# Two transformer layers on one core: VectorE jobs held back until their data has landed, sums called back one run earlier, single projections as 64x32 tiles

## The chip, the cores and the metric

The kernel runs on one core of a Trainium2 chip. The metric is the device time of one execution in microseconds (us); where several runs were made, their median. The core's engines are named as in the profile: PE (TensorE, matmuls), PEld (its weight loads), DVE (VectorE), ACT (ScalarE), POOL (GpSimd) and SP, whose queue issues the DMAs, one after the other; a DMA that must wait for a semaphore holds those behind it.

## The reference

Two equal layers are applied to x, 2048 rows of 512 numbers in float32. Each has an attention with 32 heads of width 16, whose keys and values are shared by all heads, and a dense part of width 1792 with ReLU. The weights of both layers are the same tensors.

```
def _A_ref(x, wq, wk, wv, wo):
    q = (x @ wq).reshape(B, S, H, Dh).transpose(0, 2, 1, 3)
    k = x @ wk
    v = x @ wv
    scores = jnp.einsum("bhqd,bkd->bhqk", q, k) * (Dh ** -0.5)
    p = _softmax(scores, axis=-1)
    o = jnp.einsum("bhqk,bkd->bhqd", p, v)
    return o.transpose(0, 2, 1, 3).reshape(B, S, H * Dh) @ wo

def _B_ref(x, w1, w2):
    return jnp.maximum(x @ w1, 0) @ w2

x = x + _A_ref(_layernorm(x), wq, wk, wv, wo)
x = x + _B_ref(_layernorm(x), w1, w2)
x = x + _A_ref(_layernorm(x), wq, wk, wv, wo)
x = x + _B_ref(_layernorm(x), w1, w2)
```

## The kernel before

**Units and steps.** The rows are cut into four blocks (b) of 512. The attention of a layer is cut into 32 units U (64 in all): a unit is one block's queries for four heads, eight units to a block. A unit walks over 16 key tiles (kt) of 128 keys; one unit and one key tile are a step, 1024 steps in all. Of each step `scores` makes two halves: eight matmuls of 64x32 tiles on the 512 columns of the queries into PSUM (`fst`), and one ACT call that takes the exponential of 1024 columns into `fp`. `values` then multiplies `fp` by the values into two accumulators (`facc`). Two matmuls of this kind, on the two halves of the 128 rows, and four column groups run as eight small tiles side by side; `tiles` (L263) writes one half of them.

**The end of a unit.** `keep` (L1069) adds the two accumulators into an SBUF tile `faccs` (five rotating buffers, which raw weights use too). `unit_out` (L1094) stores it to DRAM (`fod`). After an odd unit three jobs follow at fixed numbers of steps: `unit_sums` (L1101) loads the sums of the softmax (`flsum`) and the outputs (`foraw`) from there; `unit_inverse` (L1111) checks the sums on DVE, takes the reciprocal, and sends it through DRAM (`frd`) to be read back spread over the rows (`frinv`); `unit_norm` (L1125) multiplies outputs by `frinv` on DVE and splits them into two float16 parts (`fot`). Inverse and norm lie 9 and 14 steps behind the unit's end, 7 and 12 at the end of a block, 3 and 6 for unit 31 (L1447). At the end of a block `fetch` (L795) loads the rows of the residual and the first weights, and `follow` (L1394) adds that block's `chain` to the list of dense work.

**Spilled sums.** Units 32 to 41, the first of layer 1, are walked twice (`order`, L1207): over key tiles 0 to 11, and, once all are through, over 12 to 15, since the last keys of layer 1 come late. In between `spill` (L1085) stores their sums to DRAM and `recall` (L1089) loads them again; `product` (L1417) calls `recall` at the first value product of a run, and `keep` needs the sums four steps later.

**Dense work.** `chain` (L827) is the output projection, the norm (stats on DVE and POOL, halves sent through transposing DMAs), and the dense part of one block, and in layer 0 the keys and queries of layer 1 from its rows. `batch` (L268) makes two jobs at a time in 64x32 tiles, both halves of the contraction side by side in two PSUM banks (`fmisc`, which has two buffers). A job that comes alone goes another way: `mm3` (L256) makes twelve full 128x128 matmuls into one bank. Alone come the keys of each block (`key_rows`, L493, for three blocks in `following`, L712, and four in the chains of layer 0) and the queries of three groups in `following`. `key_columns` (L506) transposes the keys afterwards.

**The order of the work.** The program is written out in one order by a planner that keeps an account of the chip's time (`_Account`): each instruction and DMA is put on its engine's clock, at the end of what it needs, with modelled durations (`duration`, L132; a DMA has an issue time, a landing time LAND and bytes by FLOW, L48). `timed` (L1238) chooses by a search over the next moves whether PE next gets half a step's scores, a step's value product, or a piece of dense work, whose rate follows the due step of its chain (CHAINS, L38). Scores run at most four steps ahead of products (AHEAD). After each product, `after` (L1440) does the jobs that stand on the list of that step. One job is already held back: `unit_norm` goes to the next step while an earlier chain has not yet read `fot` (L1456). Weights come raw in the first stage: every third step from 28 on, `form` (L1401) loads one, and six steps later DVE and POOL split it into float16 parts and store it (`parts`).

A second, exact version of the net stands behind a branch at the end and is not run on these inputs.

Of the kernel before, what the change touches and what calls it, by code (L numbers as in the profile page):

```python
# [18 lines left out]
P = 128  # L19
S = 2048  # L20
D = 512
# [25 lines left out]
SIZE = {F32: 4, F32R: 4, F16: 2, I32: 4}  # L47
LAND, ISSUE, TURNED, FLOW = 1.5, 0.5, 1.25, 180e3  # L48
HOP = 0.2


class _Account:

    def __init__(self, clear=0.0):
        self.at = {"ACT": 0.0, "DVE": 0.0, "POOL": 0.0, "SP": 0.0, "PE": 0.0}
        self.slots, self.turns, self.uses = {}, {}, {}

    def place(self, t, name, bufs):
# [7 lines left out]

    def box(self, a):
        slot, pitch = self.slots.get(a.tensor.name, (None, 0))
        if slot is None:
# [17 lines left out]
    def after(self, eng, aps, writes):  # L87
        t = 0.0
        for a in aps:
            b = self.box(a)  # L90
            if b:
                for w, e, p, q, lo, hi, far, inner, end in self.uses.get(b[0], ()):
                    if (w or writes) and p < b[2] and b[1] < q and lo < b[4] and b[3] < hi:
                        if far and far == b[5] and (lo % far >= b[3] % far + b[6] or b[3] % far >= lo % far + inner):
                            continue
                        t = max(t, end + (0.0 if e == eng else HOP if e != "DMA" else 0.1))
        return t

    def note(self, eng, a, writes, end):
        b = self.box(a)  # L100
        if b:
            old = self.uses.get(b[0], [])
            floor = self.at["PE"] - 200.0
            kept = [u for u in old if u[8] > floor and not (
                (writes or not u[0] and u[1] == eng) and b[1] <= u[2] and u[3] <= b[2] and b[3] <= u[4] and u[5] <= b[4] and
                (not b[5] or b[5:] == u[6:8] and b[3] % b[5] == u[4] % b[5]))]
            self.uses[b[0]] = kept + [(writes, eng) + b[1:] + (end,)]

# [21 lines left out]


def duration(eng, op, out, ins):  # L132
    n = max(cost_of(a) for a in [out] + ins)
    psum = any(a.space == bass.MemoryType.PSUM for a in [out] + ins)
    if eng == "PE":
        n = cost_of(out)
        if op == "transpose":
            return 0.15
        c = n * (4 if ins[1].dtype == F32 else 1) / 2376.0
        return c / 8 if count(ins[0]) == 64 and cost_of(ins[0]) == 32 else c  # L140
    if eng == "ACT":
# [14 lines left out]
class _Engine:  # L156
# [4 lines left out]
    def __getattr__(self, op):  # L161
        fn = getattr(self.eng, op)

        def call(*a, **k):
# [26 lines left out]
class _Net:  # L191
# [229 lines left out]
    def forms(self):  # L421

        def wo(c):
# [3 lines left out]
            def form():  # L427
                self.until(lambda: self.exact or self.haveq[0, 3] == 4)
                self.parts(self.wo2[0][:, c], self.wo2[1][:, c], raw, 2, c)
            return form  # L430

        def w(m, f):
            raw = self.weight(m, f, False)
            return lambda: self.split(m, f, raw, False)

# [56 lines left out]

    def key_rows(self, L, b, to=None):  # L493
        nc = self.nc
# [4 lines left out]
        kop = self.kop[L][:, b * D:(b + 1) * D]  # L499
        for r in (0, 64):  # L500
            nc.vector.tensor_copy(kop[r:r + 48], kv[r:r + 48])
        for r, eng in ((32, nc.vector), (96, nc.gpsimd)):
            eng.tensor_sub(kop[r:r + DH], kv[r:r + DH], _f(kop[r:r + DH]))
        return kv

# [628 lines left out]


    def add(self, gen, size, deadline):
        self.gens.append([gen, float(size), deadline])
# [199 lines left out]
    def run(self):  # L1337
# [102 lines left out]
        def after(i):  # L1440
# [113 lines left out]
```

## Time and profile before

| | |
|---|---|
| runs, us | 2301.7, 2294.03, 2293.97; median 2294.03 |
| profiled execution, us | 2298.09 |
| its span, first to last instruction, us | 2296.3 |
| mean granted PE clock | 0.991 |
| matmuls fp x va, `facc` | 16384 records, 1130.4 us busy |
| matmuls of scores, `fst` | 16384 records, 918.8 us busy |
| ACT exponentials, 128x1024 | 2048, 1034 ns each, 1937.9 us busy |
| DMA, mean busy share of the 16 engines by queue q1 | 26.8% |

All instructions of the net are issued by one helper, so nearly every row of the profile has line L165, and groups are told apart by their tiles: out<-in, with an f in front of the program's names. A row of the timeline has the start in us from the span's start, the length, the engine, the operation and the number of instructions merged; the bracket is the engine's idle time before and what ended it. The ends of matmuls are modelled, and matmuls overlap, so PE's busy time is not PE at its peak; the time from one group's start to the next group's start is the better measure.

### The profile page before, as it was taken

How to read it: one execution, taken by the hardware profiler on the slowest of the kernel's cores; microseconds unless marked ns; L12 is line 12 of the kernel's file. 1: busy time of each engine (PE TensorE's matmuls, PEld its weight loads, DVE VectorE, ACT ScalarE, POOL GpSimd, SP SyncE). 2: the span in 40 equal slices, each digit the busy share in tenths (PEclk: the TensorE clock that was granted, in tenths of full speed). 3: DMA queues.
4: the chain of work that ended last, by engine and by line, in shares of the span. 5: the costliest groups of instructions: out<-in, count | busy, mean ns of one | idle time of the engine just before them, and what ended most of it. 6: DMA issues, size and time to landing. Idle time of an engine off the chain costs nothing.

```text
span 2296.3 us, 122379 instructions
## 1 busy us (share of the span) xinstructions
PE 2209.2 (96%) x57709; PEld 1277.0 (56%) x57709; DVE 704.2 (31%) x1533; ACT 1963.1 (85%) x2094; POOL 266.5 (12%) x311
## 2 busy tenths in 40 slices
PE   8989999999999999999899999899999999999988
PEld 4444455556566656764477754447665555555533
DVE  7433423213322233223232233332223222222242
ACT  5899999999998988777988889889999999999710
POOL 5355510001200012001010010100000000100000
PEclk9999999999999999999999999999999999999999
DMA  5344423212331133312231123432124212312032
GB/s 144 111 134 150 133 83 99 66 40 58 92 104 57 48 99 63 100 59 63 65 107 57 38 66 117 143 95 66 38 82 105 66 48 67 93 40 77 18 125 71
DMA packets 178362, 188.87 MB, mean 82 GB/s; under 512 B 79112, under 2 KB 113336, under 8 KB 177592
## 3 DMA queue, kind: packets, MB, share of 16 engines
q1 hardware_dynamic: 177848, 180.95, 26.8%
q8 instruction: 453, 7.42, 1.4%
q14 instruction: 61, 0.50, 0.1%
HBM read 116.62 MB, written 49.54 MB: 72 GB/s over the span
## 4 chain that ended last, share of the span: by engine, by line
PE 77%; ACT 13%; DMA 3%; DVE 2%; issue 2%; POOL 2%; SPq 1%; ACTq 0%; POOLq 0%; DVEq 0%
PE fmisc L165 31%; PE facc L165 30%; PE fst L165 16%; ACT fp L165 13%; DMA frinv<-frd 1%; DMA frd<-flsum 1%; DMA faccs<-fspill 1%; SPq L165 1%; POOL fxp L165 1%; POOL fbmv L165 1%; DVE fxt L165 0%; DVE fbst L165 0%; POOL fkop L165 0%; DMA out_dram<-fxt 0%; DMA fw<-fwd 0%
## 5 line engine op out<-in xcount | busy, mean ns | idle before, releaser
L165 ACT ACTIVATE fp<-fst 128x1024 f32<-128x1024 f32 x2048 | 1937.9, 1034 | 203.5 <-PE fst L165 193.8
L165 PE MATMUL facc<-fp,fva 64*32 64x512 f32 x16384 | 1130.4, 593 | 10.1 <-DVE faccs L165 6.8
L165 PE MATMUL fst<-fqop,fkop 64*32 64x512 f16 x16384 | 918.8, 378 | 41.0 <-ACT fp L165 31.3
L165 PEld LDWEIGHTS <-fkop 64*32 64x32 f16 x16384 | 387.3, 91 | 557.7 <-issue 461.0
L165 PEld LDWEIGHTS facc<-fp,fva 64*32 64x32 f32 x16384 | 364.8, 107 | 127.2 <-issue 47.5
L165 PE MATMUL fmisc<-fw,fhh 64*32 64x512 f16 (+1 forms) x6384 | 306.7, 376 | 4.5 <-DVE fseen L165 1.9
L165 PEld LDWEIGHTS <-fw 64*32 64x32 f16 (+1 forms) x9576 | 213.2, 93 | 109.4 <-issue 37.5
L165 PE MATMUL fmisc<-fxt,fw 64*32 64x512 f16 (+1 forms) x5544 | 239.0, 377 | 3.0 <-DMA fw<-fwd 2.1
L165 DVE SCALAR_TENSOR_TENSOR fxt<-fmisc,fxt 128x512 f32<-128x512 f32 x156 | 102.6, 683 | 330.4 <-PE fmisc L165 330.3
L165 PE MATMUL fmisc<-fw,fhl 64*32 64x512 f16 (+1 forms) x3192 | 202.7, 376 | 0.0
L165 POOL TENSOR_SCALAR fbmv<-fbmv 128x1 f32<-128x1 f32 x64 | 16.6, 260 | 1582.1 <-DVE fbmv L165 1581.1
L165 PEld LDWEIGHTS <-fhh 64*32 64x32 f16 (+1 forms) x6384 | 147.5, 93 | 80.5 <-issue 37.5
L165 DVE COPY fseen<-fmisc 1x1 f32<-1x1 f32 x266 | 28.9, 142 | 490.1 <-PE fmisc L165 490.0
L165 PE MATMUL fmisc<-fxq,fw 64*32 64x512 f16 x4032 | 149.6, 376 | 0.9 <-issue 0.8
L165 DVE TENSOR_SCALAR fhh<-fmisc 128x512 f16<-128x512 f32 x98 | 67.1, 685 | 218.4 <-PE fmisc L165 218.4
L165 PE MATMUL fmisc<-fwo,fot 64*32 64x512 f16 x2688 | 103.3, 376 | 0.0
L165 DVE COPY faccs<-facc 128x512 f32<-128x512 f32 x54 | 37.3, 691 | 188.8 <-PE facc L165 181.4
L165 PEld LDWEIGHTS <-fhl 64*32 64x32 f16 (+1 forms) x3192 | 74.2, 93 | 25.4 <-issue 4.9
L165 DVE SCALAR_TENSOR_TENSOR fhl<-fmisc,fhh 128x512 f16<-128x512 f32 x112 | 77.4, 691 | 35.3 <-ACT fhh L165 31.9
L165 DVE TENSOR_TENSOR faccs<-faccs,facc 128x512 f32<-128x512 f32 x96 | 65.9, 687 | 60.4 <-PE facc L165 29.7
L165 PEld LDWEIGHTS <-fot 64*32 64x32 f16 (+1 forms) x2736 | 60.4, 93 | 33.9 <-issue 9.9
L165 POOL TENSOR_TENSOR fxp<-fxn,fxp 128x512 f16<-128x512 f32 x56 | 67.8, 1230 | 27.9 <-DVE fxp L165 27.9
(112 smaller groups left out, 895.8 us busy)
## 6 DMA issues: line engine op xcount, KB each, us to landing
fw<-fwd SPq DMA_DIRECT2D x224, 256.0 KB
fod<-faccs SPq DMA_DIRECT2D x64, 256.0 KB
fqop<-fqd SPq DMA_DIRECT2D x144, 98.0 KB
fxt<-in_A_x_dram SPq DMA_DIRECT2D x32, 256.0 KB
fqd<-fqh SPq DMA_DIRECT2D x64, 128.0 KB
foraw<-fod SPq DMA_DIRECT2D x32, 256.0 KB
frinv<-frd SPq DMA_DIRECT2D x32, 256.0 KB
faccs<-in_B_w_dram SPq DMA_DIRECT2D x28, 256.0 KB
```

The lines of the kernel that those rows point to most:

```text
L165: r = fn(*a, **k)
```

## The change

- VectorE jobs that read what a DMA brings (`unit_inverse`, `unit_norm` and the split of raw weights) go to the next step's list while the account has their data landing later than 1.0 us before the time that it has reached (`early_for`, MARGIN). All jobs behind in the same list go with them.
- `recall` is also called for the next run's unit at the first product of a run, so one run earlier.
- A job that comes alone is made as 64x32 tiles into two banks, one for each half of the contraction; DVE copies the one and adds the other, and the rest reads the SBUF tile. `key_rows` goes through this way, and the single queries in `following`.
- The account: LAND 1.5 to 1.9, FLOW 180e3 to 160e3, and 0.11 us on PE when the form of a matmul changes between small tiles and full array. Its bookkeeping of uses becomes a dictionary and boxes are kept; this is left out below.

```
-LAND, ISSUE, TURNED, FLOW = 1.5, 0.5, 1.25, 180e3
-HOP = 0.2
+LAND, ISSUE, TURNED, FLOW = 1.9, 0.5, 1.25, 160e3
+HOP, SWITCH, MARGIN = 0.2, 0.11, 1.0
...
+def small(ins):
+    return count(ins[0]) == 64 and cost_of(ins[0]) == 32
...
+                if self.name == "PE":
+                    form = small(ins)
+                    if form != self.account.form:
+                        self.account.at["PE"] += SWITCH
+                    self.account.form = form
                 self.account.run(self.name, out, ins, duration(self.name, op, out, ins))
...
-        if self.exact or self.solo or self.forced or len(jobs) == 1:
+        if self.exact or self.solo or self.forced:
...
+        if len(jobs) == 1:
+            for i, (a, b) in enumerate(jobs[0][0]):
+                for h in range(2):
+                    r = slice(64 * h, 64 * h + 64)
+                    self.tiles(ps[h], a[r], b[r], i == 0, i == n - 1)
+                self.coming = n - i
+                if i < n - 1:
+                    yield 1.0
+            both = self.wt("kv", [P, D], bufs=1)
+            self.nc.vector.tensor_copy(both, ps[0])
+            self.nc.vector.tensor_add(both, both, ps[1])
+            jobs[0][1](both)
+            self.coming = 99
+            yield ("lag", 0, 1.0, self.ready((), ps))
+            return
...
     def key_rows(self, L, b, to=None):
-        nc = self.nc
-        ps = self.misc()
-        yield from self.mm3(ps, self.projection(self.wk2, slice(0, P), to or self.xt2))
-        kv = self.wt("kv", [P, D], bufs=1)
-        self.high(kv, ps)
...
+        yield from self.batch(self.key_job(L, b, to))
+        return self.kv
...
+            sq = {}
             yield from self.keys(0, b, self.homes()[b])
...
-            yield from self.queries(0, 0, [b])
+            yield from self.batch(self.query(0, 0, b, self.xt2, sq))
+            yield from self.squares(0, 0, [b], sq)
...
+    def early_for(self, fn, a):
+
+        if fn == self.unit_norm and self.outs < self.asked:
+            return True
+        tiles = self.ol[a[0]] if fn == self.unit_norm else self.ol[a[0]][1:] if fn == self.unit_inverse else getattr(
+            fn, "tiles", ())
+        return bool(tiles) and self.sim.after("DVE", tiles, False) + MARGIN > max(self.now, self.sim.at["DVE"])
...
             if self.first(i):
                 self.recall(U)
+                if run_of[i] + 1 < len(units):
+                    self.recall(units[run_of[i] + 1])
...
-                if not self.exact and jobs[0][0] == self.unit_norm and self.outs < self.asked and i + 1 < n:
+                if not self.exact and i + 1 < n and self.early_for(*jobs[0]):
                     later[i + 1] = jobs + later.get(i + 1, [])
                     break
```

`key_job` holds what stood in `key_rows` behind the matmuls (the copies and the differences of the key operand); the two weight splits in `forms` get a mark (`form.tiles = [raw]`) that names the raw tile.

More of the change, by code (lines that the diff above doesn't have):

```diff
@@ L56, in __init__ @@
         self.slots, self.turns, self.uses = {}, {}, {}
+        self.form, self.boxes = None, {}
     def place(self, t, name, bufs):
@@ L67, in box, with found @@
     def box(self, a):
+        key = a.tensor.name, a.offset, a.ap, a.dtype
+        if key not in self.boxes:
+            self.boxes[key] = self.found(a)
+        return self.boxes[key]
+    def found(self, a):
         slot, pitch = self.slots.get(a.tensor.name, (None, 0))
@@ L91, in after @@
             if b:
-                for w, e, p, q, lo, hi, far, inner, end in self.uses.get(b[0], ()):
-                    if (w or writes) and p < b[2] and b[1] < q and lo < b[4] and b[3] < hi:
+                for (w, e, p, q, lo, hi, far, inner), end in self.uses.get(b[0], {}).items():
+                    if end > t and (w or writes) and p < b[2] and b[1] < q and lo < b[4] and b[3] < hi:
                         if far and far == b[5] and (lo % far >= b[3] % far + b[6] or b[3] % far >= lo % far + inner):
@@ L101, in note @@
         if b:
[L102 to L107, printed above, removed]
+            old = self.uses.setdefault(b[0], {})
+            key = (writes, eng) + b[1:]
+            if writes and key not in old or len(old) > 48:
+                floor = self.at["PE"] - 200.0
+                for u in [u for u, t in old.items() if t < floor or writes and (
+                        b[1] <= u[2] and u[3] <= b[2] and b[3] <= u[4] and u[5] <= b[4] and
+                        (not b[5] or b[5:] == u[6:8] and b[3] % b[5] == u[4] % b[5]))]:
+                    del old[u]
+            old[key] = end
     def run(self, eng, out, ins, cost):
@@ L139, in duration @@
         c = n * (4 if ins[1].dtype == F32 else 1) / 2376.0
-        return c / 8 if count(ins[0]) == 64 and cost_of(ins[0]) == 32 else c
+        return c / 8 if small(ins) else c
     if eng == "ACT":
@@ L429, in form @@
                 self.parts(self.wo2[0][:, c], self.wo2[1][:, c], raw, 2, c)
+            form.tiles = [raw]
             return form
@@ L433, in w, with form @@
             raw = self.weight(m, f, False)
-            return lambda: self.split(m, f, raw, False)
+            def form():
+                self.split(m, f, raw, False)
+            form.tiles = [raw]
+            return form
         out = [] if self.exact else [lambda m=m, f=f: w(m, f) for f in range(NF) for m in range(2)]
```

19 lines of the change are left out of this document (13 added, 6 removed).

## The prediction, made before the change was built or timed

> **What bounds the kernel now.** I read the page first, then the chain, the list of waits, a table of windows, and the timeline around each long wait. The page and its chain:
>
> ```profile
> span 2296.3 us, 122379 instructions
> ...
> PE 2209.2 (96%) x57709; PEld 1277.0 (56%) x57709; DVE 704.2 (31%) x1533; ACT 1963.1 (85%) x2094; POOL 266.5 (12%) x311
> ...
> PE 77%; ACT 13%; DMA 3%; DVE 2%; issue 2%; POOL 2%; SPq 1%; ACTq 0%; POOLq 0%; DVEq 0%
> PE fmisc L165 31%; PE facc L165 30%; PE fst L165 16%; ACT fp L165 13%; DMA frinv<-frd 1%; DMA frd<-flsum 1%; DMA faccs<-fspill 1%; SPq L165 1%; POOL fxp L165 1%; POOL fbmv L165 1%; DVE fxt L165 0%; DVE fbst L165 0%; POOL fkop L165 0%; DMA out_dram<-fxt 0%; DMA fw<-fwd 0%
> ```
>
> The profiled execution took 2298.09 us for this span of 2296.3; the median of the runs is 2294.03, so I sum the changes against 2298.1 and take the same difference off the median. TensorE carries 77% of the chain. DVE is busy 31% of the time, so a DVE instruction costs only where somebody stands behind it. The DMAs in the chain (rinv, rd, spill) are the ones the change aims at. The list of waits says how long DVE stood on landings (total, times, longest):
>
> ```profile
> DVE foraw L165 <- DMA frinv<-frd: 53.2, 12, 8.9
> ...
> DVE faccs L165 <- DMA faccs<-fspill: 20.4, 3, 8.4
> DVE fgood L165 <- DMA flsum<-fod: 19.5, 4, 6.3
> DVE fbst L165 <- DMA faccs<-in_B_w_dram: 18.7, 6, 6.6
> ```
>
> That is 111.8 us of a waiting DVE, which is not 111.8 us of time. What counts is where TensorE or ScalarE stood too. The windows (length; then busy time of PE, PEld, DVE, ACT, POOL; the granted clock; DMA share, GB/s):
>
> ```profile
> 138.00:154.00 16.00, 12.67 (x256) 6.19 (x255) 7.17 (x18) 11.50 (x13) 8.44 (x7) 0.89 0.58 189
> 840.00:860.00 20.00, 18.07 (x337) 7.76 (x344) 5.54 (x14) 14.76 (x17) 1.59 (x1) 0.91 0.51 158
> 1072.00:1096.00 24.00, 18.40 (x321) 6.67 (x305) 9.17 (x20) 16.73 (x18) 5.53 (x8) 0.86 0.49 99
> 1440.00:1456.00 16.00, 11.84 (x248) 5.51 (x238) 4.75 (x13) 10.20 (x12) 0.00 (x0) 0.89 0.44 139
> 1100.00:1126.00 26.00, 22.39 (x497) 9.27 (x482) 3.79 (x11) 25.94 (x29) 0.33 (x1) 1.00 0.11 32
> ```
>
> ```profile
> 1520.00:2170.00 650.00, 645.05 (x18576) 376.58 (x18568) 165.93 (x366) 606.13 (x641) 16.34 (x24) 1.00 0.22 66
> ```
>
> From 1520 to 2170 PE is busy 645.05 of 650 us: nothing of this change can shorten that. In the first four windows PE and ACT both have holes and the clock is under 1.00; each holds a DVE that waits for a landing. In 1100 to 1126 DVE waits as well (its lsum wait), but ACT is busy 25.94 of 26.00, so that wait costs little.
>
> **Stalls that should go.** PE's own idle time in the four windows, and the DVE instructions that stand behind them:
>
> ```profile
> 144.64 0.66 PE L165 MATMUL facc<-fp,fva 64*32 64x512 f32 x7 [2.12 <-DVE fseen L165]
> ...
> 850.69 0.66 PE L165 MATMUL fmisc<-fident,fkv 128*128 128x128 f32 x4 [1.68 <-DVE fkv L165]
> ...
> 1086.05 1.10 PE L165 MATMUL facc<-fp,fva 64*32 64x512 f32 x7 [2.08 <-DVE faccs L165]
> ...
> 1445.03 1.89 PE L165 MATMUL facc<-fp,fva 64*32 64x512 f32 x9 [3.23 <-DVE faccs L165]
> ```
>
> ```profile
> 140.98 0.69 DVE L165 TENSOR_TENSOR foraw<-foraw,frinv 128x512 f32<-128x512 f32 x1 [8.22 <-DMA frinv<-frd]
> ...
> 848.15 0.69 DVE L165 TENSOR_TENSOR foraw<-foraw,frinv 128x512 f32<-128x512 f32 x1 [8.90 <-DMA frinv<-frd]
> ...
> 1083.50 0.71 DVE L165 TENSOR_TENSOR foraw<-foraw,frinv 128x512 f32<-128x512 f32 x1 [1.97 <-DMA frinv<-frd]
> ...
> 1085.31 0.68 DVE L165 TENSOR_TENSOR faccs<-faccs,facc 128x512 f32<-128x512 f32 x1
> ...
> 1409.01 1.48 DVE L165 TENSOR_TENSOR faccs<-faccs,facc 128x512 f32<-128x512 f32 x2 [8.39 <-DMA faccs<-fspill]
> ...
> 1424.92 1.48 DVE L165 TENSOR_TENSOR faccs<-faccs,facc 128x512 f32<-128x512 f32 x2 [4.04 <-DMA faccs<-fspill]
> ...
> 1444.28 1.48 DVE L165 TENSOR_TENSOR faccs<-faccs,facc 128x512 f32<-128x512 f32 x2 [7.98 <-DMA faccs<-fspill]
> ```
>
> At 1083.50 the pattern is plain: unit_norm stands at the head of DVE's queue for its rinv, and the add that frees PE's accumulator runs only behind it, at 1085.31; PE waits 2.08 us for that add. To each pause I add what the clock lost in its window: length times one minus the granted clock, 16 x 0.11 = 1.8, 20 x 0.09 = 1.8, 24 x 0.14 = 3.4, 16 x 0.11 = 1.8. The three unit_norm stalls then cost 2.12 + 1.8, 1.68 + 1.8 and 2.08 + 3.4 = 12.9 us; the last recall 3.23 + 1.8 = 5.0. For the two earlier recalls I take the hole that they leave in ACT:
>
> ```profile
> 1411.97 1.02 ACT L165 ACTIVATE fp<-fst 128x1024 f32<-128x1024 f32 x1 [1.55 <-PE fst L165]
> ...
> 1427.82 1.94 ACT L165 ACTIVATE fp<-fst 128x1024 f32<-128x1024 f32 x2 [1.55 <-PE fst L165]
> ```
>
> So the recalls cost 5.0 + 3.1 = 8.1 us, and both kinds 21.0.
>
> [...]
>
> Will they go? For the recalls, the DMA queue (SP) and one landing:
>
> ```profile
> 1426.83 0.42 SPq L165 DMA_DIRECT2D faccs<-fspill  x1
> ...
> 1438.60 0.42 SPq L165 DMA_DIRECT2D faccs<-fspill  x1
> ```
>
> ```profile
> 1126.13 0.59 SPq L165 DMA_DIRECT2D frinv<-frd  x1
> ```
>
> ```profile
> 1129.96 0.69 DVE L165 TENSOR_TENSOR foraw<-foraw,frinv 128x512 f32<-128x512 f32 x1 [6.08 <-DMA frinv<-frd]
> ```
>
> The recall issued at 1438.60 is used at 1444.28, 5.7 us later. One run earlier its place is that of the recall at 1426.83, 11.8 us sooner than now, and the wait is 7.98: it goes whole. It moves past one output store, the q loads and any unit sums between; each recall holds SP 0.42 us and has five rotating buffers, so I cost the move at nothing (if its buffer were still in use, the q loads behind it on SP would wait). For unit_norm the deferral depends on the account. From issue to use that rinv took 3.83 us. The old account reckons 0.5 + 1.5 + 262144/180e3 = 3.46, the new one 0.5 + 1.9 + 262144/160e3 = 4.04, and the test adds 1.0. That errs on the late side, so a DVE that is sent in is rarely early. But the account's idea of when SP gets to a DMA is also only a model, so I take 80%: 21.0 x 0.8 = 16.8 us, with bounds from 8.1 (recalls alone) to 21.0. The waits on raw weights and on lsum I cost at nothing: the cover is ACT, which stays full beside them as in 1100 to 1126; without that cover they hold at most their 38.2 us of DVE.
>
> **Key projections as tiles.** Ten single jobs change form: three keys and three queries in the first stage, four keys for layer 1. A group of scores, three full-array matmuls and the next group, against the same in tiles alone:
>
> ```profile
> 1093.60 0.41 PE L165 MATMUL fst<-fqop,fkop 64*32 64x512 f16 x8
> ...
> 1094.69 0.41 PE L165 MATMUL fst<-fqop,fkop 64*32 64x512 f16 x8
> ```
>
> ```profile
> 1436.05 0.47 PE L165 MATMUL fst<-fqop,fkop 64*32 64x512 f16 x8
> ...
> 1436.70 0.47 PE L165 MATMUL fst<-fqop,fkop 64*32 64x512 f16 x8
> ```
>
> Between the second pair lie two groups of eight tiles: 0.65 us for three groups, 0.217 each. The first pair spans four such lengths, 0.867, and takes 1.09: 0.22 us for changing form and back. Twelve matmuls cut into four give 0.9 us a job, ten jobs 8.9 at most. The planner will also run several together, and the first stage is partly waiting, so I take 5.0 (bounds 2.5 and 8.9). Against it stands the second half-sum:
>
> ```profile
> L165 DVE TENSOR_TENSOR faccs<-faccs,facc 128x512 f32<-128x512 f32 x96 | 65.9, 687 | 60.4 <-PE facc L165 29.7 <-DMA faccs<-fspill 20.4 <-ACT faccs L165 2.6
> ...
> L165 DVE COPY fkv<-fmisc 128x512 f32<-128x512 f32 x7 | 4.8, 688 | 27.7 <-PE fmisc L165 27.6
> ```
>
> The copy (0.688) stays and an add (0.687) follows, while both misc banks are held; a query's casts start behind it. Ten adds are 6.9 us at most, and nothing where scores and values fill PE meanwhile; I take 3.0.
>
> [...]
>
> **What the deferral costs.** A job sent back keeps all jobs behind it in its list: the forms' weight loads (which issue DMAs on SP), the q and residual fetches, and follow, which starts the next dense chain. Seven chains follow a unit_norm in the loop. Margin 1.0 plus half a step, for two tests (sums and norm), with a step of two ACT calls at 25.94/29 = 0.9 us: 2 x (1.0 + 0.9) x 7 = 27 us of chains starting late. In 1100 to 1126, before such a start, PE idles 26 - 22.39 = 3.6 us, 0.14 of the time: 3.7 us at most; many tests do not bind, so I take 2.0. The rest (dictionary in place of list, cached boxes) changes no instruction by itself. SWITCH adds 0.11 to the account for a change of form, about half of the 0.22 above, so plans near transposes fit better; at nothing, plus or minus 5 us because every later choice of the planner shifts.
>
> Sum: -16.8 - 5.0 + 3.0 + 2.0 = -16.8. Against the profiled execution 2298.1 - 16.8 = 2281.3, and against the median 2294.0 - 16.8 = 2277.2.
>
> **The rivals.**
> *The account misses the landings.* Three of the stalls came although norm is slotted steps after inverse; if the deferral does not trigger there, only recalls and keys are left: -8.1 - 5.0 + 5.0 = -8.1, 2286. For it: SP's queue is the least certain part of the account. Against: new constants fit the one landing above.
> *The clock dips stay.* If the clock falls for another reason than the pauses, 8.8 x 0.8 = 7.0 of the gain fails: 2284. Against: all four windows have the dip. [...]
> *More than the stalls.* If a better account keeps all 21.0, saves 8.9 on forms and costs nothing: 2294 - 30 = 2264.
> *Slower: chains start late.* If the account runs behind the chip, the tests send unit_norm back many steps and follow with it. At 0.14 us of PE per us, with the gain halved (11) and all ten adds on the path (6.9), being slower by 11.5 needs (11.5 + 11 - 6.9)/0.14 = 111 us over seven starts, 16 us or nine steps each; at 25 us each the time is 2294 - 11 + 6.9 + 24.5 = 2314. For it: follow does stand behind unit_norm. Against: the fit of the constants.
>
> **How the numbers follow.** Forecast 0.50, more 0.13, account misses 0.20, clock stays 0.08, slower 0.09. A measurement of this kernel tells about 0.5% (11.5 us) from no change, so faster means below 2282.5: 0.50 + 0.13 = 0.63. Within: 0.28. Slower: 0.09. The range goes from the larger gain, 2262, to 2296, where the low bounds (8.1 and 2.5 gained) meet the full costs (6.9 and 3.7) and 2 us of replanning; the slower rival is left out. The likeliest case alone has 2270 to 2283.
>
> **What would show it.** Right: in the profile after, DVE's wait on the spill is near zero and its wait on rinv far below 53.2; PE has no pause over 1.5 us behind faccs or fkv between 100 and 1500; no 128*128 matmul reads the key weights between scores; the clock in the old stall places is 1.00. Wrong: rinv waits of 4 us and more remain (account misses), or stretches without dense work as in 1100 to 1126 have grown (chains late), or new holes in ACT stand after the key adds.

## The result: slower, and the profile after

| | before | after |
|---|---|---|
| median, us (runs) | 2294.97 (2288.4 to 2301.7, 6) | 2317.98 (2316.15 to 2321.14, 6) |
| profiled execution, us | 2298.09 | 2316.15 |
| its span, us | 2296.3 | 2314.3 |
| mean granted PE clock | 0.991 | 0.991 |

The ratio is 1.01, with a 95% interval of 1.0081 to 1.0119: 23 us slower, where 16.8 us faster was forecast. In the changed kernel the helper that issues all instructions stands at L179 instead of L165. The six runs of before hold the three of the table further up and three more. These lines are from the page after: span, busy times and instructions, and the chain by engine.

```profile
span 2314.3 us, 124098 instructions
...
PE 2230.5 (96%) x58549; PEld 1121.7 (48%) x58549; DVE 718.7 (31%) x1547; ACT 1956.7 (85%) x2093; POOL 268.1 (12%) x311
...
PE 79%; ACT 15%; DVE 2%; issue 2%; POOL 1%; DMA 0%; SPq 0%; ACTq 0%; POOLq 0%; DVEq 0%
```

The DMAs, 3% of the chain before, have gone from it: the landings that the change aims at no longer stand in the way. PE and ACT together have taken their place and more (94% against 90%). The list of waits after (total, times, longest) says the same of the landings:

```profile
ACT fp L179 <- PE fst L179: 224.7, 311, 12.3
...
DVE foraw L179 <- DMA frinv<-frd: 24.6, 9, 6.3
DVE fbst L179 <- DMA faccs<-in_B_w_dram: 19.8, 8, 6.7
DVE fgood L179 <- DMA flsum<-fod: 13.0, 4, 4.6
```

The wait on rinv fell from 53.2 to 24.6 us and the wait on the spilled sums (20.4) is not in the list any more. But the first row has grown. Before it read:

```profile
ACT fp L165 <- PE fst L165: 193.8, 285, 12.0
```

ScalarE stood 31 us longer for scores, and more often. Some of that stands in two holes of about 10 us behind key projections (one is shown further down); the rest is spread out. The four windows in which the prediction saw the stalls (columns as there) have PE and ACT busier than before, and the clock at 1.00 (the mean of the whole run stays 0.991, with dips elsewhere now, such as 0.89 from 1380 to 1396):

```profile
138.00:154.00 16.00, 14.92 (x384) 7.17 (x375) 8.06 (x20) 15.96 (x19) 9.63 (x8) 1.00 0.63 207
840.00:860.00 20.00, 18.97 (x474) 8.81 (x460) 11.98 (x26) 19.21 (x21) 8.19 (x12) 1.00 0.57 123
1072.00:1096.00 24.00, 20.66 (x532) 9.33 (x525) 13.59 (x30) 20.79 (x24) 6.93 (x11) 1.00 0.37 77
1440.00:1456.00 16.00, 15.24 (x397) 8.19 (x389) 7.52 (x17) 15.51 (x18) 2.08 (x2) 1.00 0.56 178
```

So the loss lies elsewhere. Two stretches that had no stall, first before:

```profile
600.00:800.00 200.00, 199.95 (x5880) 129.67 (x5872) 56.40 (x124) 181.85 (x194) 10.30 (x14) 1.00 0.24 69
1520.00:2100.00 580.00, 575.13 (x16570) 339.16 (x16562) 150.59 (x333) 540.08 (x572) 16.34 (x24) 1.00 0.24 70
```

and after:

```profile
600.00:800.00 200.00, 197.89 (x5688) 101.19 (x5680) 56.25 (x121) 175.82 (x187) 12.34 (x16) 1.00 0.24 69
1520.00:2100.00 580.00, 576.69 (x16229) 298.83 (x16221) 149.13 (x326) 527.14 (x559) 16.34 (x24) 1.00 0.22 68
```

PE's busy time is the same from 1520 to 2100 (575.13 and 576.69 of 580), the clock is 1.00 in both, and still PE started 341 matmuls fewer and ACT made 559 calls instead of 572: 13 calls at 580/572 = 1.01 us each are 13 us in 580. The shorter stretch says the same (187 calls against 194). Busy time doesn't show this loss, the counts do: the ends of matmuls are modelled, and in the rows below one of 0.41 us has its next start after 0.33 in place of 0.22, and PE still counts as busy. Where it goes is seen in the timeline after, a few microseconds of such a stretch, first ACT and then PE:

```profile
1940.23 2.04 ACT L179 ACTIVATE fp<-fst 128x1024 f32<-128x1024 f32 x2
1942.69 4.69 ACT L179 ACTIVATE fp<-fst 128x1024 f32<-128x1024 f32 x5 [0.42 <-PE fst L179]
```

```profile
1941.14 0.41 PE L179 MATMUL fmisc<-fw,fhl 64*32 64x512 f16 x8
1941.35 1.05 PE L179 MATMUL facc<-fp,fva 64*32 64x512 f32 x16
1942.21 0.41 PE L179 MATMUL fst<-fqop,fkop 64*32 64x512 f16 x8
1942.43 0.63 PE L179 MATMUL fmisc<-fw,fhh 64*32 64x512 f16 x16
...
1945.27 0.41 PE L179 MATMUL fmisc<-fw,fhh 64*32 64x512 f16 x8
1945.60 0.41 PE L179 MATMUL fst<-fqop,fkop 64*32 64x512 f16 x8
```

ACT is done at 1942.27 and then stands dry, with no scores ready: the matmuls of the next ones start only at 1942.21, because dense work and a value product were put ahead of them. The group has its length of 0.22 (1942.21 to 1942.43), and ACT begins at 1942.69, 0.26 us behind the group's end; 0.42 us of ACT are gone. Later PE pays in its turn: from 1945.27 to 1945.60 a group takes 0.33 instead of 0.22. It looks as if the planner took ACT to begin right at the end of the matmuls.

And so its account does reckon. This is the part of the diff that the prediction passed over as bookkeeping, in the account's `after`, which finds the time from which an instruction may start:

```
-                for w, e, p, q, lo, hi, far, inner, end in self.uses.get(b[0], ()):
-                    if (w or writes) and p < b[2] and b[1] < q and lo < b[4] and b[3] < hi:
+                for (w, e, p, q, lo, hi, far, inner), end in self.uses.get(b[0], {}).items():
+                    if end > t and (w or writes) and p < b[2] and b[1] < q and lo < b[4] and b[3] < hi:
...
                         t = max(t, end + (0.0 if e == eng else HOP if e != "DMA" else 0.1))
```

`end > t` looks like a shortcut past uses that can't matter. But `t` holds the HOP of 0.2 us from an earlier use already, and `end` doesn't hold its own. A group of scores is eight tiles of 512/2376/8 = 0.027 us in the account. The first tile sets t to its end + 0.2; the last ends 7 x 0.027 = 0.19 later, which is under t, and is skipped. ACT is reckoned to start 0.2 - 0.19 = 0.01 us behind the last tile instead of 0.2. Written out from the two programs' accounts: where ACT is dry, before starts it 0.20 behind the last tile 477 times, after 0.01 behind it 383 times.

The account against the chip, at the end of the ACT calls of three steps (chip minus account, us; the chip's times counted from the trace's ACT calls, two a step):

| step | before | after |
|---|---|---|
| 192 | 13.6 | 10.1 |
| 640 | 34.3 | 43.1 |
| 992 | 50.2 | 62.9 |

Before, the chip falls behind in jumps, at the stalls (steps 640 to 672 alone 10). After, the jumps are smaller, but it falls behind everywhere: the median over stretches of 16 steps is 0.8 us, against 0.2 before.

### The profile page after: what moved, and what is told of

It reads as the page before. It is cut to its first block, busy times and chain, and to the rows that moved or that the text cites. A ratio compares the mean times of both kernels' runs of the same rounds, so it can differ in the third digit from the quotient of the medians.

```text
span 2314.3 us, 124098 instructions
## 1 busy us (share of the span) xinstructions
PE 2230.5 (96%) x58549; PEld 1121.7 (48%) x58549; DVE 718.7 (31%) x1547; ACT 1956.7 (85%) x2093; POOL 268.1 (12%) x311
## 4 chain that ended last, share of the span: by engine, by line
PE 79%; ACT 15%; DVE 2%; issue 2%; POOL 1%; DMA 0%; SPq 0%; ACTq 0%; POOLq 0%; DVEq 0%
PE fmisc L179 31%; PE facc L179 31%; PE fst L179 17%; ACT fp L179 15%; POOL fbmv L179 1%; DVE fxt L179 0%; DVE fbst L179 0%; POOL fxp L179 0%; DVE fgood L179 0%; POOL fkop L179 0%; DMA fxq<-fxp 0%; DVE fkv L179 0%; DVE fxp L179 0%; DMA faccs<-in_A_wk_dram 0%; DVE faccs L179 0%
## 5 line engine op out<-in xcount | busy, mean ns | idle before, releaser
L179 ACT ACTIVATE fp<-fst 128x1024 f32<-128x1024 f32 x2048 | 1931.4, 1037 | 232.8 <-PE fst L179 224.7
L179 PE MATMUL facc<-fp,fva 64*32 64x512 f32 x16384 | 1097.2, 591 | 2.0 <-DVE fva L179 1.6
L179 PE MATMUL fst<-fqop,fkop 64*32 64x512 f16 x16384 | 856.3, 380 | 43.4 <-ACT fp L179 34.1
L179 PEld LDWEIGHTS <-fkop 64*32 64x32 f16 x16384 | 370.6, 91 | 652.1 <-issue 552.3
L179 PEld LDWEIGHTS facc<-fp,fva 64*32 64x32 f32 x16384 | 326.3, 106 | 145.7 <-issue 52.9
L179 PE MATMUL fmisc<-fw,fhh 64*32 64x512 f16 (+1 forms) x6384 | 315.2, 376 | 2.2 <-DVE fseen L179 2.2
L179 PEld LDWEIGHTS <-fw 64*32 64x32 f16 (+1 forms) x9576 | 177.0, 93 | 132.1 <-issue 40.4
L179 PE MATMUL fmisc<-fxt,fw 64*32 64x512 f16 (+1 forms) x5544 | 232.8, 376 | 2.9 <-issue 2.1
L179 DVE SCALAR_TENSOR_TENSOR fxt<-fmisc,fxt 128x512 f32<-128x512 f32 x156 | 102.6, 683 | 338.4 <-PE fmisc L179 338.4
L179 POOL TENSOR_SCALAR fbmv<-fbmv 128x1 f32<-128x1 f32 x64 | 16.6, 260 | 1601.0 <-DVE fbmv L179 1600.0
L179 PE MATMUL fmisc<-fw,fhl 64*32 64x512 f16 (+1 forms) x3192 | 185.3, 376 | 0.0
L179 DVE COPY fseen<-fmisc 1x1 f32<-1x1 f32 x266 | 28.3, 141 | 502.4 <-PE fmisc L179 502.3
L179 PEld LDWEIGHTS <-fhh 64*32 64x32 f16 (+1 forms) x6384 | 117.1, 93 | 96.0 <-issue 38.3
L179 PE MATMUL fmisc<-fxq,fw 64*32 64x512 f16 x4032 | 150.3, 376 | 0.2
L179 DVE TENSOR_SCALAR fhh<-fmisc 128x512 f16<-128x512 f32 x98 | 67.2, 686 | 257.3 <-PE fmisc L179 257.3
L179 PE MATMUL fmisc<-fwo,fot 64*32 64x512 f16 x2688 | 100.0, 376 | 0.0
L179 DVE COPY faccs<-facc 128x512 f32<-128x512 f32 x55 | 38.0, 692 | 175.6 <-PE facc L179 172.5
L179 DVE SCALAR_TENSOR_TENSOR fhl<-fmisc,fhh 128x512 f16<-128x512 f32 x112 | 77.5, 692 | 33.9 <-ACT fhh L179 30.6
L179 DVE TENSOR_TENSOR faccs<-faccs,facc 128x512 f32<-128x512 f32 x96 | 65.9, 687 | 54.4 <-PE facc L179 45.0
L179 PEld LDWEIGHTS <-fhl 64*32 64x32 f16 (+1 forms) x3192 | 57.4, 93 | 33.5 <-issue 1.7
L179 POOL TENSOR_TENSOR fxp<-fxn,fxp 128x512 f16<-128x512 f32 x56 | 67.6, 1227 | 27.9 <-DVE fxp L179 27.9
L179 PEld LDWEIGHTS <-fot 64*32 64x32 f16 (+1 forms) x2736 | 51.5, 93 | 38.7 <-issue 12.3
```

The costliest lines, as they stand in the source:

```text
L179: r = fn(*a, **k)
```

## The experiments

The theory: the skipped HOP costs the time, by making ACT and PE wait for each other by tenths of a microsecond, hundreds of times, and the rest of the change does about what was predicted. The rivals: the tiles of single keys cost more than their form saves; the jobs sent back, or the new constants, spoil the order of the dense work. Ratios are to the kernel before on the same chip, with their 95% intervals. The runs with the deferral, the tiles or the constants alone are the changed kernel with everything else taken back and the condition taken out; with all parts taken back in this way its planner writes the order of the kernel before, instruction for instruction, so they can be read as the kernel before with one part.

**The shortcut taken out of the changed kernel.**

```
-                    if end > t and (w or writes) and p < b[2] and b[1] < q and lo < b[4] and b[3] < hi:
+                    if (w or writes) and p < b[2] and b[1] < q and lo < b[4] and b[3] < hi:
```

> The changed kernel, but the account's search compares a use's end without the new shortcut (a use is no longer skipped because its bare end lies before the time found so far, which already holds a 0.2 us hop). Shortcut theory: in the account of the changed kernel ScalarE starts 0.01 us after a score group's last tile instead of 0.20, so the planner sends scores too late or too early by up to 0.19 us wherever ScalarE had run dry, and the chip falls behind the account by about 0.75 us per 16 steps outside all stalls. With the hop restored that drip goes (before has none): 256 steps from step 640 to 896 then take within 1 us of what the account says, and the whole 2283 to 2292 us, faster than both kernels or level with the first. Tile theory: the single jobs as tiles with their added VectorE add, two banks held, and the deferral cost the time everywhere; the shortcut is bookkeeping: 2310 to 2320.

Measured: 2284.7 us, 0.9955 (0.9937 to 0.9973); this is the repaired kernel of the text below. The one condition is worth 33 us in the whole change (1.01 against 0.9955). From 1520 to 2100 the window, and the wait of ACT for scores:

```profile
1520.00:2100.00 580.00, 573.46 (x16423) 344.17 (x16413) 146.47 (x323) 538.65 (x570) 16.34 (x24) 1.00 0.23 67
```

```profile
ACT fp L179 <- PE fst L179: 183.7, 281, 12.0
```

ACT's calls are back at 570, and its wait is down from 224.7 to 183.7. The chip is now 5.3, 19.2 and 28.9 us behind the account at steps 192, 640 and 992, and the median over 16 steps is back at 0.2. The expectation for steps 640 to 896 missed: they take 7 us more than the account says and not within 1, because jumps are left.

**The shortcut alone, put into the kernel before.** The list stays a list; only the condition is added.

```
-                    if (w or writes) and p < b[2] and b[1] < q and lo < b[4] and b[3] < hi:
+                    if end > t and (w or writes) and p < b[2] and b[1] < q and lo < b[4] and b[3] < hi:
```

> The kernel before with one added condition in the account: a use whose bare end lies before the time found so far is skipped. No other part of the change. Shortcut theory: the same slow drip as in the changed kernel, some 20 to 28 us over the run with all of the old stalls still there: 2312 to 2325. Tile theory: as before, 2290 to 2300.

Measured: 2322.98 us, 1.0114 (1.0091 to 1.0136), span 2322.6 against 2296.3. No job of this kernel does anything that it didn't do before; its order is different, and that costs 26 us. The same two rows show it: calls down from 572 to 566, ACT's wait up from 193.8.

```profile
1520.00:2100.00 580.00, 575.65 (x16281) 293.87 (x16275) 151.65 (x330) 532.13 (x566) 20.69 (x29) 1.00 0.24 70
```

```profile
ACT fp L165 <- PE fst L165: 225.3, 317, 12.5
```

The chip is 15.5, 54.0 and 80.8 us behind the account at the three steps: the stalls and the drip together.

**The shortcut kept, but not for ScalarE behind TensorE.** This asks which handoff it is.

```
-                    if end > t and (w or writes) and p < b[2] and b[1] < q and lo < b[4] and b[3] < hi:
+                    if (end > t or eng == "ACT" and e == "PE") and (w or writes) and p < b[2] and b[1] < q and lo < b[4] and b[3] < hi:
```

> The changed kernel whole, its shortcut kept for all pairs of engines except ScalarE waiting for TensorE, where the hop is reckoned in full. If the loss is the start of ScalarE alone (0.01 us reckoned, 0.20 before, 0.32 on the chip), this is level with the run that has the shortcut gone: 0.994 to 0.998. If VectorE's and GpSimd's waits for tiles matter as well, it lies between that and the changed kernel: 1.000 to 1.006.

Measured: 2289.1 us, 0.9976 (0.9964 to 0.9987), against 0.9955 without the shortcut and 1.01 with it. So most of the loss is ScalarE's start behind the scores: with this one pair reckoned in full the chip's time is nearly that without the shortcut. What all other handoffs add is 0.2% by the medians, and the two intervals overlap (0.9964 to 0.9973), so it may be nothing; the ends of the intervals allow 0.5%.

**A larger HOP.** If 0.2 is too little, since ACT began 0.26 behind the group in the rows above (the median over the 311 waits for scores in the profile after is 0.32), a larger one should gain. This is the repaired kernel with full-array keys (below) and

```
-HOP, SWITCH, MARGIN = 0.2, 0.11, 1.0
+HOP, SWITCH, MARGIN = 0.32, 0.11, 1.0
```

> Full-array keys, hop restored, and the hop made 0.32 us in place of 0.20: in the trace of the changed kernel ScalarE, when dry, starts 0.32 us behind the last tile of its scores. Dose test of the hop theory: 0.01 costs 25 us, 0.20 is good; if the account only has to be right, 0.32 is as good or better (0.986 to 0.993) and the chip falls behind the account less than with 0.20 outside stalls. If an account that is too slow costs as well, since the hop is charged to every pair of engines and 0.32 was seen for one pair: 0.995 to 1.005.

Measured: 2293.25 us, 0.9999 (0.9986 to 1.0012), against 0.9921 with 0.2. The chip now runs ahead of its account (10.0, 12.7 and 17.5 us at the three steps), and the order is no good either. 0.01 costs 33 us (with the keys as tiles) and 0.32 costs 18. The list of waits doesn't show this loss: ACT waits 164.5 us for scores, less than the 182.7 with 0.2. It shows in the time that the exponentials cover, 23.5 us more for the same number of calls of the same length, so they overlap less (2048 x 1.036 - 1961.6 = 160 us, against 2048 x 1.035 - 1938.1 = 182). First with 0.2, then with 0.32:

```profile
L179 ACT ACTIVATE fp<-fst 128x1024 f32<-128x1024 f32 x2048 | 1938.1, 1035 | 193.3 <-PE fst L179 182.7 <-ACT fp L179 1.1
L179 ACT ACTIVATE fp<-fst 128x1024 f32<-128x1024 f32 x2048 | 1961.6, 1036 | 180.2 <-PE fst L179 164.5 <-ACT fp L179 0.9
```

One thing was left as it is in every run. The search of `timed` looks ahead with a constant of its own for the same handoff, `TO_ACT = 0.2`. With HOP at 0.2 the account and the search agree; at 0.01 and at 0.32 they don't (at 0.32 the account has ACT dry 1011 times, at 0.2 517 times, while on the chip ACT waits for scores 286 and 288 times). So the runs show that a wrong handoff in the account costs time. Whether it costs because the account then differs from the chip, or because it differs from the search, they don't show; a run with both constants changed together would.

**Recalls one run earlier, alone.** The kernel before, with only

```
                 self.recall(U)
+                if run_of[i] + 1 < len(units):
+                    self.recall(units[run_of[i] + 1])
```

> The kernel before with only the sums called back one run earlier. Both theories: the three waits of VectorE on the spill go, 20.4 us to under 2, and with them 6 to 8 us of time: 2287 to 2289. If another wait takes their place (the q loads behind the moved recalls on the DMA queue), 2293 to 2297.

Measured: 2288.0 us, 0.9963 (0.9945 to 0.9981), 9.7 us below the 2297.7 of before in that comparison by the medians, 8.5 by the ratio. The spill isn't in its list of waits. By the ends of ACT's calls in the two profiles it gains 1.8, 1.9 and 5.9 us in steps 648 to 656, 656 to 664 and 664 to 672, where the three recalls stand (priced 1.55, 1.55 and 5.0). Its window in the last recall's place, which before had PE at 11.84, ACT at 10.20 and the clock at 0.89:

```profile
1440.00:1456.00 16.00, 14.12 (x361) 7.32 (x360) 8.64 (x22) 15.60 (x18) 2.08 (x2) 1.00 0.45 140
```

**The deferral alone.** The kernel before with `early_for`, the marks on the raw tiles and the test:

```
-                if not self.exact and jobs[0][0] == self.unit_norm and self.outs < self.asked and i + 1 < n:
+                if not self.exact and i + 1 < n and self.early_for(*jobs[0]):
```

> The kernel before with the deferral alone (margin 1.0, old constants, hop right, full-array keys, no earlier recall). The prediction's three unit_norm stalls, 12.9 us at 80%, less 2 for chains that start late: 0.994 to 0.997. With the recall's 8.5 us put to it this should give the run with old constants (0.990), which asks for 0.993 to 0.994 here. If deferral does little by itself: 0.998 to 1.001.

Measured: 2280.41 us, 0.9935 (0.9919 to 0.995), 14.1 us below its 2294.55. The waits that it was to take away and to leave:

```profile
DVE foraw L179 <- DMA frinv<-frd: 24.8, 9, 6.1
...
DVE faccs L179 <- DMA faccs<-fspill: 15.6, 2, 8.1
```

The second line is what it leaves, the spill. And the window of the stall at 850.69, which before had ACT at 14.76 and the clock at 0.91:

```profile
840.00:860.00 20.00, 19.45 (x472) 11.82 (x471) 5.87 (x14) 19.19 (x21) 1.60 (x1) 1.00 0.43 144
```

By the ends of ACT's calls it gains 4.9, 3.8 and 3.8 us in steps 48 to 56, 400 to 416 and 496 to 512, where the three stalls stand: 12.5 of the 12.9 that were priced. Not all of this is the deferral's. Steps 48 to 56 are 5.2 us shorter with the tiles alone and with the constants alone too, and steps 400 to 416 are 1.4 to 2.2 us shorter there: a new order alone can move a stall away. At the third place those two runs gain only 1.3 and 1.1.

**Full-array keys again, in the repaired kernel.** The first run without the shortcut, and a job that comes alone by `mm3` as before:

```
-        if self.exact or self.solo or self.forced:
+        if self.exact or self.solo or self.forced or len(jobs) == 1:
```

> As the first of these runs (no shortcut), but single jobs stay full-array matmuls into one bank, as before. If tiles save the form changes as predicted (5 us less 3), this is 2 us slower than the first run. If their latency costs more than the form changes (in the changed kernel ScalarE has a hole of 9.8 us at 80 us and one of 10.7 us at 1389 us, each behind a key projection, where before had at most 2.9), this is 6 to 12 us faster than the first run: 2273 to 2284.

Measured: 2279.45 us, 0.9921 (0.9902 to 0.994), so the tiles cost 0.34% or 8 us inside the change; the two intervals touch (0.9937 to 0.994), and the next run shows the cost more clearly.

**The tiles alone, in the kernel before** (`batch`, `key_rows`, `key_job` and the single queries of the change; the account as it was):

> The kernel before with one part alone: single jobs as 64x32 tiles with the added VectorE add (hop right, old constants, no deferral, no earlier recall). The prediction has 5 us of form changes saved and 3 us of latency: 0.997 to 1.000. If the latency is the larger, as the holes behind the key projections in the changed kernel suggest: 1.002 to 1.005.

Measured: 2304.21 us, 1.0043 (1.0029 to 1.0057): 10 us slower. Where it can be seen best is the first stage. ACT, before:

```profile
67.95 2.86 ACT L165 ACTIVATE fp<-fst 128x1024 f32<-128x1024 f32 x3 [0.23 <-PE fst L165]
72.43 7.79 ACT L165 ACTIVATE fp<-fst 128x1024 f32<-128x1024 f32 x8 [1.62 <-PE fst L165]
```

and with the tiles alone:

```profile
66.06 5.61 ACT L179 ACTIVATE fp<-fst 128x1024 f32<-128x1024 f32 x6 [0.21 <-PE fst L179]
80.90 3.77 ACT L179 ACTIVATE fp<-fst 128x1024 f32<-128x1024 f32 x4 [9.23 <-PE fst L179]
```

while DVE there does this:

```profile
76.21 0.69 DVE L179 COPY fkv<-fmisc 128x512 f32<-128x512 f32 x1 [4.76 <-PE fmisc L179]
77.00 0.69 DVE L179 TENSOR_TENSOR fkv<-fkv,fmisc 128x512 f32<-128x512 f32 x1
77.73 0.88 DVE L179 CAST fkop<-fkv 48x512 f16<-48x512 f32 x2
```

The next scores need these keys. A hole of 1.62 us became one of 9.23, and the add at 77.00 stands in the way of the keys' casts. Most of this hole is given back (step 32 comes 7 us later than before, step 64 1.5 us); the rest of the 10 us grows slowly, 3.8 by step 512 and 8.6 by step 832, in stretches without a hole of its own, and no run says by which step of the planner.

**The old rule for unit_norm, in the repaired kernel with full-array keys.**

```
-                if not self.exact and i + 1 < n and self.early_for(*jobs[0]):
+                if not self.exact and jobs[0][0] == self.unit_norm and self.outs < self.asked and i + 1 < n:
```

> The kernel with full-array keys and the hop restored (0.992 of before), and now also without the deferral of VectorE jobs: recall one run earlier and the new constants are all that is left of the change. If the deferral takes away the three unit_norm stalls as the prediction had it (12.9 us, 80% of it), this run is 8 to 13 us slower than that kernel, 0.996 to 0.998 of before. If those stalls are also avoided by the new plan or cost little, it is level with it: 0.991 to 0.994.

Measured: 2283.36 us, 0.9946 (0.9932 to 0.996), against 0.9921: in this company the deferral gives 0.25%, less than its 14 us alone, and the intervals overlap. Two of the three windows tell a part of why: without the deferral the third stall is back, but the first is not, since this order avoids it.

```profile
138.00:154.00 16.00, 14.96 (x377) 7.25 (x376) 7.17 (x16) 15.96 (x19) 12.41 (x10) 1.00 0.63 201
1072.00:1096.00 24.00, 19.79 (x323) 6.32 (x313) 7.54 (x15) 18.39 (x21) 4.07 (x6) 0.86 0.35 81
```

**The old constants alone taken back there** (deferral, recall and full-array keys stay):

```
-LAND, ISSUE, TURNED, FLOW = 1.9, 0.5, 1.25, 160e3
-HOP, SWITCH, MARGIN = 0.2, 0.11, 1.0
+LAND, ISSUE, TURNED, FLOW = 1.5, 0.5, 1.25, 180e3
+HOP, SWITCH, MARGIN = 0.2, 0.0, 1.0
```

> Full-array keys, hop restored, deferral and recall kept, but LAND 1.5, FLOW 180e3 and no SWITCH as before. If the constants matter through the deferral (a landing reckoned 0.4 to 0.6 us too early is covered by the margin of 1.0), nothing changes: 0.990 to 0.995. If they place the first stage better, this run loses in the first 32 steps (before has 107 us there, the new constants 106): still the same within 3 us. If the old constants bring waits of VectorE on landings back: 0.995 to 0.998.

Measured: 2271.13 us, 0.9896 (0.9881 to 0.9912), the fastest version of this study, 24 us below before and 47 below after, and a little under all that was expected. Its window from 1520 and two of its waits:

```profile
1520.00:2100.00 580.00, 575.17 (x16560) 344.55 (x16552) 147.11 (x326) 543.43 (x575) 16.35 (x24) 1.00 0.22 67
```

```profile
ACT fp L179 <- PE fst L179: 168.5, 276, 13.6
...
DVE foraw L179 <- DMA frinv<-frd: 26.9, 11, 6.6
```

ACT makes 575 calls in the stretch, and the sum of its waits for scores is lower than in all other runs but the one with the HOP of 0.32.

**The new constants alone, in the kernel before** (LAND 1.9, FLOW 160e3 and SWITCH 0.11, with the two lines that apply it):

> The kernel before with the account's constants alone (LAND 1.9, FLOW 160e3, SWITCH 0.11; hop right). The runs with full-array keys differ by 6 us in disfavour of the new constants (2277 against 2271 when both are put on a before of 2295). If that difference is the constants', this run is 3 to 9 us slower than before: 1.001 to 1.004. If it came from how the constants meet the deferral's margin (landings reckoned late and the margin on top), it is level or faster: 0.995 to 1.000.

Measured: 2290.49 us, 0.9984 (0.9972 to 0.9995): 4 us faster, as in the second case of what was expected. So the 6 us that they seem to cost beside the deferral (0.9921 against 0.9896, with intervals that share 0.9902 to 0.9912) are not in the constants themselves. The repaired kernel with full-array keys waits 36.6 us on rinv with the new ones and 26.9 with the old ones, so they did not help the deferral; why is open.

## Why the prediction was wrong, point by point

**The step that failed** is this sentence: "The rest (dictionary in place of list, cached boxes) changes no instruction by itself." It does not, and it changes the order of most of them. In that rest stood a new condition, and the prediction asked what a faster lookup does, not whether it returns the same times. Alone it costs 26 us, within the change 33. The diff shows `end` without HOP on one side of the comparison and `t` with HOP on the other; worked out from the account's own 0.027 us a tile, this was to be had before any run. The dictionary and the boxes themselves do nothing: without the condition and every other part the order of before comes out again. The prediction's allowance for later choices of the planner, plus or minus 5 us, stood beside the constants and was a fifth of what this one condition moved.

Put in a ladder of the runs that hold several parts (each ratio minus one, times 2295). The ratios come from separate comparisons, and the steps of 6 and 8 us are between intervals that touch; the step of 33 is far clear of them:

| kernel | against before, us | by the last part |
|---|---|---|
| deferral and recalls, keys and constants as before | -24 | |
| with the new constants | -18 | +6 |
| with keys as tiles | -10 | +8 |
| with the shortcut: the change | +23 | +33 |

**The stalls.** Forecast -16.8, bounds -8.1 and -21.0. Measured -24 together, -14 and -10 alone. For the recalls the mechanism was right: they were priced at 8.1 and gave 8.5 to 9.7, at the three places named. The three unit_norm stalls were priced at 12.9, and the deferral gave 14.1 with 24.8 us of waiting on rinv left. Here the size is partly luck, as the first stall also goes in two runs without the deferral, and only the third is clearly its own. The 80% and its upper bound were too careful.

**The clock.** The 8.8 us of granted clock (1.8 + 1.8 + 3.4 + 1.8) were counted to the pauses. The recalls alone bring the window 1440 to 1456 from 0.89 to 1.00, with PE busy 14.12 us in place of 11.84; the deferral alone brings 840 to 860 from 0.91 to 1.00, with 19.45 in place of 18.07. The pauses there were 3.23 and 1.68 us; the dips went with them, and the rival that the dips stay is out. But a pause of this length doesn't bring a dip each time. The first of these pauses is in the kernel before, the second in the run with the shortcut alone, where the first stall still stands; under each is the window around it, with the clock at 1.00:

```profile
923.94 0.83 PE L165 MATMUL fmisc<-fxt,fw 64*32 64x512 f16 x20 [2.08 <-DMA fw<-fwd]
918.00:930.00 12.00, 9.92 (x289) 5.51 (x280) 6.05 (x11) 7.93 (x9) 0.00 (x0) 1.00 0.69 238
```

```profile
145.01 0.66 PE L165 MATMUL facc<-fp,fva 64*32 64x512 f32 x7 [2.03 <-DVE fseen L165]
138.00:154.00 16.00, 12.63 (x288) 5.20 (x273) 7.18 (x18) 13.10 (x16) 8.27 (x8) 1.00 0.57 186
```

So the prediction's step from four windows to a dip for each pause was too strong: what decides whether a dip comes is not shown.

**The tiles.** Forecast -5.0 for changes of form and +3.0 for the added adds. Measured +8 within the change and +10 alone: the sign was wrong. The forecast let scores and values fill PE while DVE copies and adds; in the first stage the scores waited for those keys, and ACT stood for 9.23 us with the tiles alone. The prediction's upper price, 6.9 for all ten adds, went the right way and was still too small; what the rest is made of was not found. In the trace the copy and the add, 0.69 us each, stand ahead of the keys' casts.

**What the deferral costs.** Forecast +2.0 for chains that start late, and the slower rival was built on it. The deferral alone came out better than the stalls' price, so no such cost shows. The result landed near the rival's 2314 by luck, since its mechanism is not the one at work: the run without the shortcut keeps every deferral and is 33 us faster, and the stretch without dense work that starts near 1100 is 29 us long before and 28 after. ACT and PE miss each other by tenths of a microsecond, hundreds of times.

**The constants.** "At nothing, plus or minus 5": -4 alone, +6 beside the deferral; the size was about right, and the sign seems to depend on the company.

**The signs named.** The spill gone from the waits, rinv far below 53.2, no full-array matmul on key weights between scores and the clock of 1.00 in the old places: these came true in a kernel that is slower. That PE has no pause over 1.5 us behind faccs or fkv did not. Two stand at a key projection, in a window with the clock at 0.89:

```profile
1380.87 0.63 PE L179 MATMUL fmisc<-fxt,fwkh 64*32 64x512 f16 x16 [1.80 <-DVE faccs L179]
1385.23 0.65 PE L179 MATMUL fmisc<-fident,fkv 128*128 128x128 f32 x4 [1.57 <-DVE fkv L179]
```

```profile
1380.00:1396.00 16.00, 12.18 (x300) 5.64 (x308) 5.01 (x12) 6.45 (x7) 1.59 (x1) 0.89 0.19 60
```

Of the signs for the wrong case two came true. Two waits on rinv over 4 us remain, 6.3 at 257.2 and 5.8 at 1136.3. And "new holes in ACT stand after the key adds", here in the changed kernel:

```profile
1365.35 12.59 ACT L179 ACTIVATE fp<-fst 128x1024 f32<-128x1024 f32 x13
1388.60 1.02 ACT L179 ACTIVATE fp<-fst 128x1024 f32<-128x1024 f32 x1 [10.65 <-PE fst L179]
```

with the copy and the add of the keys between them:

```profile
1383.69 0.69 DVE L179 COPY fkv<-fmisc 128x512 f32<-128x512 f32 x1 [3.06 <-PE fmisc L179]
1384.48 0.69 DVE L179 TENSOR_TENSOR fkv<-fkv,fmisc 128x512 f32<-128x512 f32 x1
```

A hole of that size at this place is in none of the repaired kernel, the one with the tiles alone and the one with the shortcut alone (their longest near it are 3.20, 2.65 and 2.90), so it takes the shortcut together with another part of the change. All signs had been chosen at the old stalls and at the parts that were priced; none looked at a stretch without stalls, where the loss was. The prediction had said of the stretch with PE busy 645.05 of 650 us that nothing could shorten it; it didn't ask what could lengthen it, and 13 us in 580 were lost there.

**A sum.** The range's lower end is 2262, while the larger gain that it is taken from comes to 2264; no term accounts for the 2 us, and nothing hangs on them.

## What to carry to other kernels

Where a model of the chip decides the order of the work, an edit to that model is an edit to every instruction: price it by what the model returns for the commonest handoff, before and after, and count a stretch that has no stall. Two times that are compared must both hold the handoff or both lack it. When busy time and clock agree and the kernel is slower, compare the number of calls in the same stretch.

## What the runs showed that was not expected

- A handoff from PE to ACT that the account reckons at 0.01 us in place of 0.20 costs 26 to 33 us over 2048 calls, and one at 0.32 costs 18 us. ACT began 0.26 us behind the length of its score group in the rows shown; and yet the order written with 0.20 beats that with 0.32. The search's own 0.2, which never changed, is a possible reason.
- PE pauses of 1.68 to 3.23 us came with a lower granted clock in four windows before (0.86 to 0.91 over 16 to 24 us), and two others of 2.03 and 2.08 us came with 1.00.
- A change of the order alone can take a stall away that another change was meant for: 5.2 us in steps 48 to 56 with the tiles alone and with the constants alone.
- PE's busy time can agree to 0.3% (575.13 and 576.69 us) while 2% fewer matmuls start.
